# A fused block-sparse attention and feed-forward kernel: one token a partition in the loads of q and k for the later two thirds of batch 0

## The chip, the cores and the metric

The kernel runs on one core of a Trainium2 chip. The core has five engines that run their own instruction streams side by side: TensorE (PE in the profile, with its weight loads as PEld), VectorE (DVE), ScalarE (ACT), GpSimd (POOL) and SyncE (SP), which here only issues DMAs. Sixteen DMA engines move data between the device's memory and the core's on-chip memory (SBUF); TensorE writes its results to a second on-chip memory (PSUM). The metric is device time in microseconds, the median of several runs. A profiled execution of the same program gives the trace.

## The reference

Two parts follow each other. The first is causal attention with block selection over 4 batches, 8 heads, 768 tokens and head size 64: for each token the three best of twelve blocks of 64 keys are chosen by the product of q with the blocks' mean keys, and the token's own block is always in. The second is a feed-forward layer with the tanh form of GELU.

```
k_rep = k.reshape(B, H, n_blocks, block, D).mean(axis=3)
gate_scores = np.einsum('bhsd,bhnd->bhsn', q, k_rep)      # later blocks: -1e9
top_idx = np.argsort(gate_scores, axis=-1)[..., -top_k:]  # top_k = 3, and the own block
scores = scale * np.matmul(q, k.transpose(0, 1, 3, 2))    # masked by block and causally
attn = softmax(scores)
x = (attn @ v), heads side by side                        # 3072 x 512
h = x @ w_in                                              # 512 -> 2048
out = gelu_tanh(h) @ w_out                                # 2048 -> 512
```

The sums of the block means and the choice of blocks need more precision than half precision gives, so q and k also enter in a high and a low half-precision part.

## The kernel before

All work is cut into named steps, and one long list, `ORDER` (L26 to L127), says in which order they are emitted. Each engine runs its own instructions in that order; semaphores hold an instruction until what it reads is there and what it overwrites has been read. A suffix such as `:p`, `:a` or `:v` puts a copy on POOL, ACT or DVE; `@0` to `@2` chooses one of three wide PSUM tiles; `dm4` emits four matmuls without use that keep TensorE's clock up. No planner runs when the program is built: the list is fixed text.

Batch 0 is treated apart from the other three. Its 8 heads form two groups `g` of four heads (two pairs of heads `j` each), and its 768 tokens form three chunks `c` of 256 tokens, each of two token tiles of 128. For chunk 0, `load_first` (L349, steps `d0.g.t.x`) brings q, k and v of one token tile and four heads into a third each of an io tile: partition = token, one run of 64 floats for each head. For chunks 1 and 2, the later two thirds, `load_two` (L365, steps `dd.g.c.x`) brings q (x = 0) or k (x = 1) of all 256 tokens of a chunk in one DMA: partition p gets tokens 2p and 2p + 1, which lie side by side in memory, so that a run is 128 floats. `part` (L386, steps `r.g.c.x`) then copies this on POOL or ACT into a tile of the pool `w32`, sorted by even and odd token. `load_v` (L377, steps `d0.g.t.2`) brings v of one token tile into the last third of one of these io tiles. There are nine io tiles (pool `io`); an io tile is used again when all that it holds has been read.

`t_in` (L432, steps `t2.g.c`) transposes q and k of a chunk on TensorE, eight transposes of 128 x 128, into one wide PSUM tile. For chunks 1 and 2 the even and the odd tokens are written with a stride of two, which puts the tokens in order again. Then `hi` (L451, `h2`, ACT) makes the scaled half-precision copy, `q_low` (`l`, DVE) the low part of q, `k_sum0` and `k_block0` (`s`, `b`, DVE) the block sums, `gate0` and `select0` (`g`, PE; `m`, DVE) the choice of blocks, `mask_t0` and `mask_c0` (`mt`, `mc`) the transposed mask. Scores (`k`, `ma`, PE), exponentials (`x`, ACT), the causal cut (`a`, POOL), the products with v (`p`, PE), their normalisation (`n`, DVE) and the transposes back (`xt`, `xc`) follow for each chunk.

In between, the weights come in: sixteen loads of 512 KB each (`lw.in.s`, `lw.out.s`, L320) into tiles of the pool `w32`, which has seven of 512 KB, each cast to half precision on POOL or DVE (`cw`, L332). The tiles of `part` are from the same pool. The first loads of batches 1 to 3 (`d.4.0`: q of head pair 4; `d.4.1`: k of pair 4) and their half-precision parts (`hn`, `ln`) are in the opening too. The feed-forward layer runs in twelve chunks of 256 tokens: `u` (L931, PE, `hps`), `y` (GELU on ACT), `f` (L965, PE, `ops` and `pso`), `o` and `w` (copy and store). Its matmuls are mixed with the attention of later batches.

SP issues nearly all DMAs, in the order of the list; ACT issues four at the start (k of chunk 0). Eight semaphores serve all DMAs in turn: a DMA waits until the eighth before it has landed, which is why the length of SP's list matters beside its contents.

Of the kernel before, what the change touches and what calls it, by code (L numbers as in the profile page):

```python
# [8 lines left out]
FP32 = mybir.dt.float32  # L9
# [15 lines left out]

ORDER = """  # L26
d0.0.0.0 d0.0.1.0 d0.0.0.1 c.bd c.e0 c.ident d0.0.1.1 c.e.3:p c.gate dd.0.1.0 dd.0.1.1 d0.1.1.0
d0.1.0.0 c.e.2:v d0.1.0.1 r.0.1.0:p dm20 t2.0.0@0 r.0.1.1:p d0.1.1.1 c.m0.0 dd.1.1.0 d0.0.1.2
c.m0.1 c.ident16 h2.0.0 s.0.0 dm14 t2.0.1@1 h2.0.1 b.0.0 dd.1.1.1 l.0.0 s.0.1 g.0.0 c.own t2.1.0@2
h2.1.0 lw.in.5 d0.1.1.2 m.0.0 s.1.0 c.e.1:p dm9 mt.0.0 l.1.0 r.1.1.0:a mc.0.0:a b.1.0 r.1.1.1:p  # L30
c.v.0 k.0.0.0.0@0 dm16 k.0.0.1.0@2 ma.0.0.0 dm3 g.1.0 l.0.1 x.0.0.1.0 d0.0.0.2 m.1.0 dm7 t2.1.1@1
dm8 mt.1.0 a.0.0.1 v.0.0.1:p x.0.0.0.0 a.0.0.0 mc.1.0:a b.0.1 dm8 g.0.1 k.1.0.0.0@2 s.1.1 c.bi
h2.1.1 v.0.0.0:a d0.0.3.2 k.1.0.1.0@0 d0.1.0.2 lw.in.0 cw.in.0:p dd.1.2.0 lw.out.0 ma.1.0.0
x.1.0.1.0 m.0.1 dm16 k.0.1.0.1@0 x.1.0.0.0 c.v.1 dm11 mt.0.1 p.0.0.0@2 p.0.0.1 l.1.1 dd.0.2.0
p.0.0.3 dd.0.2.1 lw.in.4 d0.1.3.2 p.0.0.2 dm3 k.0.1.1.1@1 a.1.0.0 mc.0.1:a a.1.0.1 ma.0.1.1 b.1.1
v.1.0.0:p cw.in.5:p r.0.2.0:p lw.in.7 v.1.0.1:a n.0.0 lw.in.1 g.1.1 r.0.2.1:p x.0.1.0.1 x.0.1.1.1
r.1.2.0:p cw.in.4:p dm7 k.0.1.0.0@0 k.0.1.1.0@2 ma.0.1.0 m.1.1 t2.0.2@1 x.0.1.0.0 s.0.2 dm11 mt.1.1
p.1.0.0@0 p.1.0.2 p.1.0.3 x.0.1.1.0 p.1.0.1 dd.1.2.1 d0.0.2.2 n.1.0 mc.1.1:a k.1.1.1.1@2 cw.in.1:p
dm2 xt.0.0 r.1.2.1:p h2.0.2 lw.out.1 dm9 k.1.1.0.1@0 xc.0.0:a a.0.1.0 lw.in.3 v.0.1.0:p cw.out.0:p
cw.in.3:p l.0.2 ma.1.1.1 lw.in.2 d0.1.2.2 d.4.0 x.1.1.0.1 xt.1.0 x.1.1.1.1 lw.out.2 xc.1.0:v  # L40
t2.1.2@1 cw.in.2:p u.0.0.0@0 u.0.0.1 lw.in.6 lw.out.4 b.0.2 s.1.2 u.0.2.0@2 h2.1.2 l.1.2 g.0.2
b.1.2 u.0.2.1 y.0.0 u.0.1.0@1 m.0.2 u.0.1.1 k.1.1.0.0@0 y.0.2 v.0.1.1:p d.4.1 lw.out.3 v.1.1.0:a
c.par.0 y.0.1 k.1.1.1.0@2 mt.0.2 cw.in.7:p a.0.1.1 a.1.1.1 hn0.4.0:p ma.1.1.0 p.0.1.0@1 p.0.1.2
cw.out.1:p mc.0.2:v ln0.4.0:v p.0.1.3 p.0.1.1 g.1.2 d0.0.4.2 x.1.1.1.0 x.1.1.0.0 f.0.0.0 n.0.1
k.0.2.1.0@1 k.0.2.0.0@2 ma.0.2.0 d.5.0 a.1.1.0 d0.1.4.2 x.0.2.0.0 v.1.1.1:p p.1.1.0@0 m.1.2 p.1.1.2
p.1.1.1 p.1.1.3 xt.0.1 k.0.2.0.1@2 n.1.1 x.0.2.1.0 hn1.4.0:p cw.out.2:p cw.in.6:p cw.out.3:v
xc.0.1:a k.0.2.1.1@1 ma.0.2.1 zql.4.0 mt.1.2 x.0.2.0.1 v.0.2.0:v mc.1.2:v k.0.2.1.2@0 f.0.0.1
xt.1.1 zqh.4.0 u.0.3.0@2 xc.1.1:v x.0.2.1.1 d.5.1 hn0.5.0:p ln1.4.0:v lw.out.6 d0.0.5.2 ln0.5.0:v
k.0.2.0.2@1 ma.0.2.2 u.0.3.1 x.0.2.0.2 lw.out.5 x.0.2.1.2 s.4.0 b.4.0 u.1.0.0@1 u.1.1.0@0
c.ke.0.0:p g.4.0 y.0.3 lw.out.7 u.1.0.1 u.1.1.1 zql.5.0 cw.out.4:v m.4.0 zqh.5.0 zkh.4.0 u.1.2.0@2  # L50
u.1.2.1 hn1.5.0:p a.0.2.1 y.1.0 a.0.2.0 k.1.2.0.0@1 ln1.5.0:v d0.1.5.2 y.1.1 v.0.2.1:a c.ke.0.1:p
cw.out.5:v k.1.2.1.0@0 cw.out.6:p ma.1.2.0 y.1.2 x.1.2.1.0 c.par.1 s.5.0 b.5.0 x.1.2.0.0 p.0.2.0@2
# [78 lines left out]
def kernel(  # L131
# [9 lines left out]
    nc = tc.nc  # L141
    B, H, S, D = q.shape
# [21 lines left out]
    io = ctx.enter_context(tc.tile_pool(name="io", bufs=9))  # L164
    w32p = ctx.enter_context(tc.tile_pool(name="w32", bufs=7))
# [11 lines left out]
    copy_on = {"a": nc.scalar.copy, "v": nc.vector.tensor_copy,  # L177
               "p": nc.gpsimd.tensor_copy}
# [12 lines left out]
    def step(name, f, *args):  # L191
        assert name not in steps, name
        steps[name] = (f, args)
# [3 lines left out]
    ident32 = const.tile([128, 128], FP32)  # L197
# [149 lines left out]
    IO = {}  # L347
# [14 lines left out]
        )  # L362
        IO["v", g, t] = IO["first", g, t][:, 2]

    def load_two(g, c, x):  # L365

        a = io.tile([128, 3, 2, 128], FP32, tag="io", name=f"io_{g}_{c}_{x}")
        nc.sync.dma_start(
            out=a[:, 0:2].rearrange("p a j (h w) -> p (a j h w)",
                                    w=64).rearrange("p (h w) -> p h w", h=4),  # L370
            in_=(q, k)[x][0, 4 * g:4 * g + 4,
                          c * 256:(c + 1) * 256].rearrange(
                "h (p s) d -> p h (s d)", s=2),
        )
        IO["two", g, c, x] = a

    def load_v(g, t):  # L377
        a = IO["two", g, t // 2, t % 2]
        nc.sync.dma_start(
            out=a[:, 2].rearrange("p j (h d) -> p (j h) d", d=D),  # L380
            in_=v[0, 4 * g:4 * g + 4, t * 128:(t + 1) * 128].rearrange(
                "h p d -> p h d"),
        )
        IO["v", g, t] = a[:, 2]

    def part(g, c, x, eng):  # L386

        if ("part", g, c) not in IO:
            IO["part", g, c] = w32p.tile([128, 2, 512], FP32, tag="w32",
                                         name=f"w32_q_{g}_{c}")  # L390
        copy_on[eng](
            out=IO["part", g, c][:, x].rearrange("p (s h d) -> p h s d",
                                                 s=2, d=D),
            in_=IO["two", g, c, x][:, 0:2].rearrange(
                "p a j (h w) -> p (a j h w)", w=64).rearrange(
                "p (h s d) -> p h s d", h=4, d=D))

    def load(p, x):
        b, hp = divmod(p, HP)
# [32 lines left out]
    def t_in(g, c):  # L432

        w = wide.tile([128, 1024], FP32, tag=f"wide{at_slot[0]}",
                      name=f"w_{g}_{c}")
        for x in range(2):
            for j in range(2):
                o = j * 512 + x * 256
                for y in range(2):
                    if c == 0:  # L440
                        to = w[:, o + y * 128:o + (y + 1) * 128]
                        src = IO["first", g, y][:, x, j]
                    else:
                        to = w[:, o:o + 256].rearrange("d (p s) -> d s p",
                                                       s=2)[:, y]
                        src = IO["part", g, c][:, x, y * 256 + j * 128:
                                               y * 256 + (j + 1) * 128]
                    nc.tensor.transpose(to, src, ident32)
        U["w", g, c] = w

    def hi(g, c):  # L451
# [233 lines left out]
    for c in range(NSL2):  # L685
        for g in range(NG):
            un = f"{g}.{c}"
            step(f"t2.{un}", t_in, g, c)
            step(f"h2.{un}", hi, g, c)
            step(f"l.{un}", q_low, g, c)  # L690
            step(f"s.{un}", k_sum0, g, c)
            step(f"b.{un}", k_block0, g, c)
            for y in range(2):
                step(f"v.{un}.{y}", v_copy0, g, c, y)
            step(f"g.{un}", gate0, g, c)
            step(f"m.{un}", select0, g, c)
            step(f"mt.{un}", mask_t0, g, c)
            step(f"mc.{un}", mask_c0, g, c)
            for i in range(c + 1):
                for j in range(2):  # L700
                    step(f"k.{un}.{j}.{i}", score0, g, c, j, i)
                    step(f"x.{un}.{j}.{i}", expo0, g, c, j, i)
                step(f"ma.{un}.{i}", mask_add0, g, c, i)
            for j in range(2):
                step(f"a.{un}.{j}", causal0, g, c, j)
                for hh in range(2):
                    step(f"p.{un}.{2 * j + hh}", pv0, g, c, j, hh)
            step(f"n.{un}", normalise, (g, c), 4, un)
            step(f"xt.{un}", x_t, (g, c), 4, un)
            step(f"xc.{un}", x_c0, g, c)  # L710
# [357 lines left out]
```

## Time and profile before

| | |
|---|---|
| median of 3 runs | 278.28 us (277.52 to 278.75) |
| profiled execution | 277.6 us |
| its span, first to last instruction | 275.0 us |
| PE busy | 261.8 us (95%) |
| ACT, DVE, POOL busy | 190.6, 135.8, 131.3 us |
| mean granted clock of TensorE | 0.994 |
| DMA | 42.65 MB in 114,416 packets |

The page of the profile gives busy time, a picture of the span in forty slices of 6.9 us, the DMA queues, the chain of work that ended last, the costliest groups of instructions and the DMA issues. Further views are read from the trace: the chain in order of time, the instructions of an engine in order of time (start, duration, engine, line, operation, tiles, and in brackets how long the engine was idle before and what released it), the instructions of one line or tile, and tables by window. In such a table a row has the window, its length, and for PE, PEld, DVE, ACT and POOL the busy time and the number of instructions, then the granted clock, the mean busy share of the DMA engines (which may be over 1 as packets overlap) and GB/s. Times in the views are microseconds from the start of the span. An engine's idle time only matters where the chain passes through it.

### The profile page before, as it was taken

The numbers are of one execution on the slowest core, as the hardware profiler recorded it, in microseconds if no ns is written. First come the engines' busy times: TensorE is split into PE (matmuls) and PEld (weight loads), VectorE is DVE, ScalarE is ACT, GpSimd is POOL, SyncE is SP. The second block draws the span as 40 slices with busy tenths as digits, with TensorE's granted clock in tenths as the row PEclk, the third lists the DMA queues.
The fourth block names the chain that finished last, engine by engine and source line by source line (L and its number), as shares of the span: only waits on it lengthen the run. The fifth ranks groups of instructions, "written<-read, shape, count | busy, mean of one in ns | idle before, by whom it ended". The sixth has DMA issues, their size and how long they took to land.

```text
span 275.0 us, 6896 instructions
## 1 busy us (share of the span) xinstructions
PE 261.8 (95%) x2774; PEld 181.4 (66%) x2774; DVE 135.8 (49%) x427; ACT 190.6 (69%) x218; POOL 131.3 (48%) x193
## 2 busy tenths in 40 slices
PE   5889696999999999999999999999999999999995
PEld 3456583774788557795776666786675767756663
DVE  2697359787697776665546456653252110011010
ACT  1568487797889988959899877987978553512321
POOL 6547698899843679673447657600272200000000
PEclk9999799999999999999999999999999999999999
DMA  7999999999799997999996999912205211100203
GB/s 175 274 262 275 336 267 260 224 216 212 140 166 213 201 229 155 170 241 174 147 214 151 204 210 185 223 27 57 69 21 88 69 38 41 38 38 2 76 0 114
DMA packets 114416, 42.65 MB, mean 155 GB/s; under 512 B 102993, under 2 KB 107345, under 8 KB 114385
## 3 DMA queue, kind: packets, MB, share of 16 engines
q1 hardware_dynamic: 112272, 41.70, 72.2%
q10 hardware_dynamic: 2112, 0.52, 1.0%
q8 instruction: 21, 0.34, 0.6%
q14 instruction: 11, 0.08, 0.1%
HBM read 27.26 MB, written 6.29 MB: 122 GB/s over the span
## 4 chain that ended last, share of the span: by engine, by line
PE 74%; DMA 9%; ACT 5%; DVE 4%; POOL 3%; SPq 3%; issue 1%; DVEq 0%; POOLq 0%; ACTq 0%
PE hps L941 27%; PE ops L977 23%; PE st L836 8%; PE pv L878 5%; DMA w_in<-in_moe_w_in_dram 5%; PE pso L977 3%; DMA io<-in_k_dram 3%; DMA io<-in_q_dram 1%; SPq L407 1%; PE mt L814 1%; ACT qk L454 1%; ACT at L852 1%; PE kp L749 1%; PE pv L646 1%; PE gt L778 1%
## 5 line engine op out<-in xcount | busy, mean ns | idle before, releaser
L941 PE MATMUL hps<-xT,w_in 128*128 128x256 f16 x768 | 92.9, 274 | 0.0
L977 PE MATMUL ops<-w_out,gT 128*128 128x512 f16 (+1 forms) x352 | 85.0, 371 | 0.5 <-POOL w_out L338 0.5
L941 PEld LDWEIGHTS <-w_in 128*128 128x128 f16 x768 | 74.6, 98 | 14.9 <-issue 0.2
L852 ACT ACTIVATE at<-st 128x1024 f16<-128x1024 f32 (+1 forms) x72 | 62.8, 917 | 13.2 <-PE st L836 12.0
L951 ACT ACTIVATE gT<-hps 128x1024 f16<-128x1024 f32 x48 | 47.6, 1023 | 28.1 <-PE hps L941 27.7
L977 PEld LDWEIGHTS <-gT 128*128 128x128 f16 x400 | 36.8, 97 | 32.8 <-issue 1.5
L866 POOL TENSOR_SCALAR_AFFINE_SELECT at<-at 128x256 f16<-128x256 f16 x72 | 32.0, 461 | 54.1 <-ACT at L852 53.6
L185 POOL TENSOR_SCALAR hn<-io 128x768 f16<-128x768 f32 x15 | 33.5, 2232 | 9.9 <-DMA io<-in_k_dram 5.5
L836 PE MATMUL st<-qk 76*128 76x128 f16 (+2 forms) x192 | 36.2, 305 | 0.6 <-ACT at L852 0.5
L723 DVE SCALAR_TENSOR_TENSOR ln<-io,hn 128x768 f16<-128x768 f32 x24 | 24.9, 1036 | 3.0 <-POOL hn L185 2.8
L990 DVE COPY osb<-ops 128x512 f32<-128x512 f32 (+1 forms) x7 | 4.4, 632 | 42.7 <-PE ops L977 42.6
L619 ACT ACTIVATE at<-st 128x768 f16<-128x768 f32 (+1 forms) x24 | 20.7, 915 | 6.9 <-PE st L600 6.8
L836 PEld LDWEIGHTS <-qk 76*128 76x128 f16 x192 | 16.6, 97 | 12.2 <-issue 1.1
L878 PEld LDWEIGHTS <-at 128*128 128x128 f16 x504 | 17.3, 97 | 2.5 <-issue 0.4
L878 PE MATMUL pv<-v,at 128*128 128x65 f16 x504 | 17.8, 193 | 0.1
L1016 PE MATMUL dm<-zsrc 128*128 128x512 f16 (+3 forms) x40 | 11.3, 390 | 3.1 <-POOL zsrc L231 3.1
L951 ACT ACT_TABLE_LOAD x11 | 14.1, 1283 | 0.2
L742 POOL COPY qk<-khT 64x768 f16<-64x768 f16 x14 | 11.7, 838 | 1.8 <-DMA khT<-hn 1.3
L657 DVE RECIPROCAL zrec<-pv 128x12 f32<-128x12 f32 x12 | 2.8, 230 | 19.6 <-PE pv L878 19.5
L454 ACT ACTIVATE qk<-w 128x1024 f16<-128x1024 f32 x6 | 6.2, 1029 | 8.2 <-DVE ks L470 4.3
L661 DVE TENSOR_TENSOR xn<-pv,zrec 128x768 f16<-128x768 f32 x12 | 11.5, 957 | 0.4
L823 DVE COPY qk<-mt 12x640 f16<-12x640 f16 x15 | 7.3, 486 | 8.3 <-PE mt L814 8.1
(142 smaller groups left out, 311.9 us busy)
## 6 DMA issues: line engine op xcount, KB each, us to landing
io<-in_q_dram SPq DMA_DIRECT2D x24, 192.0 KB, 4.3
io<-in_k_dram SPq DMA_DIRECT2D x24, 192.0 KB, 3.9
w_in<-in_moe_w_in_dram SPq DMA_DIRECT2D x8, 512.0 KB, 6.3
w_out<-in_moe_w_out_dram SPq DMA_DIRECT2D x8, 512.0 KB, 7.0
out_dram<-osb SPq DMA_DIRECT2D x15, 256.0 KB, 2.6
w_v<-in_v_dram SPq DMA_DIRECT2D x16, 192.0 KB, 4.0
out_dram<-w_o SPq DMA_DIRECT2D x8, 256.0 KB, 2.3
io<-in_v_dram SPq DMA_DIRECT2D x12, 128.0 KB, 5.3
```

What stands on the lines that cost most here:

```text
L185: math_on[eng].tensor_scalar(out=out, in0=in_, scalar1=c, scalar2=None, op0=ALU.mult)
L619: nc.scalar.activation(out=ov, in_=iv, func=AF.Exp, bias=0.0, scale=SCALE / (QS * QS))
L661: nc.vector.tensor_tensor(out=xn[:, 0:nt].rearrange("p c h d -> p h c d"), in0=pz[:, :, :, 0:64], in1=zrec[:, :, 0:nt].unsqueeze(3).to_bro ...
L723: math_on[eng].scalar_tensor_tensor(out=g.rearrange("p t c -> p (t c)"), in0=IO[p, x].rearrange("p t h d -> p (t h d)"), scalar=QS, in1=U[ ...
L742: copy_on[eng](out=dst[0:64, :], in_=U["qh" if x == 0 else "kh", p][64 * hh:64 * hh + 64])
L836: nc.tensor.matmul(st[:, hh, cb:cb + nq * 128], kt[p % 2][hh][0:64 + NBLK, jc * 128:(jc + 1) * 128], qt[p % 2][hh][0:64 + NBLK, qc * 128:( ...
L852: nc.scalar.activation(out=ov, in_=iv, func=AF.Exp, bias=0.0, scale=SCALE / (QS * QS))
L866: nc.gpsimd.affine_select(out=a, in_=a, compare_op=ALU.is_ge, fill=0.0, base=0, pattern=[[0, 2], [1, 128]], channel_multiplier=-1,)
L878: nc.tensor.matmul(U["pv", p][:, o:o + 65], AT[p, hh, jc, qc], v16[p % NSLOT][:, jc, hh, :], start=(jc == 0), stop=(jc == qc),)
L941: nc.tensor.matmul(hps[:, j * TCH:(j + 1) * TCH], w_in16[:, ci, fi * 128:(fi + 1) * 128], xT[:, ci, t0:t0 + TCH], start=(ci == 0), stop=(c ...
L951: nc.scalar.activation(out=g.rearrange("p a w -> p (a w)"), in_=G["h", ch, dj], func=AF.Gelu_apprx_tanh, bias=0.0, scale=1.0,)
L977: nc.tensor.matmul(G["o", ch, ti][:, a:b], G["g", ch, dj][:, j, row * 128:(row + 1) * 128], w_out16[:, fi, a:b], start=(fi == 0), stop=(fi ...
```

## The change

`load_two` now makes one io tile for each token tile: it loads q and then k of one token tile and four heads with two DMAs, one token a partition, as `load_first` does. The steps keep their names: `dd.g.c.y` stands where `dd.g.c.x` stood and loads token tile 2c + y. `load_v` adds v to the same tile. `part`, its eight steps `r.g.c.x` and its four tiles of pool `w32` are gone, and `t_in` reads every chunk from the io tiles and writes it without the stride. The list `ORDER` is the old one without the eight `r` steps. Lines after the list move up by one, those after `part` by nineteen.

```diff
-    def load_two(g, c, x):
-
-        a = io.tile([128, 3, 2, 128], FP32, tag="io", name=f"io_{g}_{c}_{x}")
-        nc.sync.dma_start(
-            out=a[:, 0:2].rearrange("p a j (h w) -> p (a j h w)",
-                                    w=64).rearrange("p (h w) -> p h w", h=4),
-            in_=(q, k)[x][0, 4 * g:4 * g + 4,
-                          c * 256:(c + 1) * 256].rearrange(
-                "h (p s) d -> p h (s d)", s=2),
-        )
-        IO["two", g, c, x] = a
+    def load_two(g, c, y):
+
+        t = 2 * c + y
+        a = io.tile([128, 3, 2, 128], FP32, tag="io", name=f"io_{g}_{t}")
+        for x in range(2):
+            nc.sync.dma_start(
+                out=a[:, x].rearrange("p j (h d) -> p (j h) d", d=D),
+                in_=(q, k)[x][0, 4 * g:4 * g + 4,
+                              t * 128:(t + 1) * 128].rearrange(
+                    "h p d -> p h d"),
+            )
+        IO["first", g, t] = a
 
     def load_v(g, t):
-        a = IO["two", g, t // 2, t % 2]
+        a = IO["first", g, t]
...
-    def part(g, c, x, eng):
-
-        if ("part", g, c) not in IO:
-            IO["part", g, c] = w32p.tile([128, 2, 512], FP32, tag="w32",
-                                         name=f"w32_q_{g}_{c}")
-        copy_on[eng](
-            out=IO["part", g, c][:, x].rearrange("p (s h d) -> p h s d",
-                                                 s=2, d=D),
-            in_=IO["two", g, c, x][:, 0:2].rearrange(
-                "p a j (h w) -> p (a j h w)", w=64).rearrange(
-                "p (h s d) -> p h s d", h=4, d=D))
...
                 step(f"dd.{g}.{c}.{x}", load_two, g, c, x)
-                step(f"r.{g}.{c}.{x}", part, g, c, x)
...
                 for y in range(2):
-                    if c == 0:
-                        to = w[:, o + y * 128:o + (y + 1) * 128]
-                        src = IO["first", g, y][:, x, j]
-                    else:
-                        to = w[:, o:o + 256].rearrange("d (p s) -> d s p",
-                                                       s=2)[:, y]
-                        src = IO["part", g, c][:, x, y * 256 + j * 128:
-                                               y * 256 + (j + 1) * 128]
-                    nc.tensor.transpose(to, src, ident32)
+                    nc.tensor.transpose(
+                        w[:, o + y * 128:o + (y + 1) * 128],
+                        IO["first", g, 2 * c + y][:, x, j], ident32)
```

More of the change, by code (lines that the diff above doesn't have):

```diff
@@ L27 @@
 d0.0.0.0 d0.0.1.0 d0.0.0.1 c.bd c.e0 c.ident d0.0.1.1 c.e.3:p c.gate dd.0.1.0 dd.0.1.1 d0.1.1.0
[L28 to L49, printed above, removed]
+d0.1.0.0 c.e.2:v d0.1.0.1 dm20 t2.0.0@0 d0.1.1.1 c.m0.0 dd.1.1.0 d0.0.1.2 c.m0.1 c.ident16 h2.0.0
@@ new lines @@
+s.0.0 dm14 t2.0.1@1 h2.0.1 b.0.0 dd.1.1.1 l.0.0 s.0.1 g.0.0 c.own t2.1.0@2 h2.1.0 lw.in.5 d0.1.1.2
+m.0.0 s.1.0 c.e.1:p dm9 mt.0.0 l.1.0 mc.0.0:a b.1.0 c.v.0 k.0.0.0.0@0 dm16 k.0.0.1.0@2 ma.0.0.0 dm3
+g.1.0 l.0.1 x.0.0.1.0 d0.0.0.2 m.1.0 dm7 t2.1.1@1 dm8 mt.1.0 a.0.0.1 v.0.0.1:p x.0.0.0.0 a.0.0.0
+mc.1.0:a b.0.1 dm8 g.0.1 k.1.0.0.0@2 s.1.1 c.bi h2.1.1 v.0.0.0:a d0.0.3.2 k.1.0.1.0@0 d0.1.0.2
+lw.in.0 cw.in.0:p dd.1.2.0 lw.out.0 ma.1.0.0 x.1.0.1.0 m.0.1 dm16 k.0.1.0.1@0 x.1.0.0.0 c.v.1 dm11
+mt.0.1 p.0.0.0@2 p.0.0.1 l.1.1 dd.0.2.0 p.0.0.3 dd.0.2.1 lw.in.4 d0.1.3.2 p.0.0.2 dm3 k.0.1.1.1@1
@@ new lines @@
+a.1.0.0 mc.0.1:a a.1.0.1 ma.0.1.1 b.1.1 v.1.0.0:p cw.in.5:p lw.in.7 v.1.0.1:a n.0.0 lw.in.1 g.1.1
+x.0.1.0.1 x.0.1.1.1 cw.in.4:p dm7 k.0.1.0.0@0 k.0.1.1.0@2 ma.0.1.0 m.1.1 t2.0.2@1 x.0.1.0.0 s.0.2
+dm11 mt.1.1 p.1.0.0@0 p.1.0.2 p.1.0.3 x.0.1.1.0 p.1.0.1 dd.1.2.1 d0.0.2.2 n.1.0 mc.1.1:a
+k.1.1.1.1@2 cw.in.1:p dm2 xt.0.0 h2.0.2 lw.out.1 dm9 k.1.1.0.1@0 xc.0.0:a a.0.1.0 lw.in.3 v.0.1.0:p
+cw.out.0:p cw.in.3:p l.0.2 ma.1.1.1 lw.in.2 d0.1.2.2 d.4.0 x.1.1.0.1 xt.1.0 x.1.1.1.1 lw.out.2
+xc.1.0:v t2.1.2@1 cw.in.2:p u.0.0.0@0 u.0.0.1 lw.in.6 lw.out.4 b.0.2 s.1.2 u.0.2.0@2 h2.1.2 l.1.2
@@ new lines @@
+g.0.2 b.1.2 u.0.2.1 y.0.0 u.0.1.0@1 m.0.2 u.0.1.1 k.1.1.0.0@0 y.0.2 v.0.1.1:p d.4.1 lw.out.3
+v.1.1.0:a c.par.0 y.0.1 k.1.1.1.0@2 mt.0.2 cw.in.7:p a.0.1.1 a.1.1.1 hn0.4.0:p ma.1.1.0 p.0.1.0@1
+p.0.1.2 cw.out.1:p mc.0.2:v ln0.4.0:v p.0.1.3 p.0.1.1 g.1.2 d0.0.4.2 x.1.1.1.0 x.1.1.0.0 f.0.0.0
+n.0.1 k.0.2.1.0@1 k.0.2.0.0@2 ma.0.2.0 d.5.0 a.1.1.0 d0.1.4.2 x.0.2.0.0 v.1.1.1:p p.1.1.0@0 m.1.2
+p.1.1.2 p.1.1.1 p.1.1.3 xt.0.1 k.0.2.0.1@2 n.1.1 x.0.2.1.0 hn1.4.0:p cw.out.2:p cw.in.6:p
+cw.out.3:v xc.0.1:a k.0.2.1.1@1 ma.0.2.1 zql.4.0 mt.1.2 x.0.2.0.1 v.0.2.0:v mc.1.2:v k.0.2.1.2@0
@@ L50 @@
+f.0.0.1 xt.1.1 zqh.4.0 u.0.3.0@2 xc.1.1:v x.0.2.1.1 d.5.1 hn0.5.0:p ln1.4.0:v lw.out.6 d0.0.5.2
+ln0.5.0:v k.0.2.0.2@1 ma.0.2.2 u.0.3.1 x.0.2.0.2 lw.out.5 x.0.2.1.2 s.4.0 b.4.0 u.1.0.0@1 u.1.1.0@0
 c.ke.0.0:p g.4.0 y.0.3 lw.out.7 u.1.0.1 u.1.1.1 zql.5.0 cw.out.4:v m.4.0 zqh.5.0 zkh.4.0 u.1.2.0@2
```

## The prediction

> **What bounds the kernel now.** I read the page first (busy times and slices of the span), then the chain of work that ended last in order of time, then the first 50 us engine by engine.
>
> ```profile
> span 275.0 us, 6896 instructions
> PE 261.8 (95%) x2774; PEld 181.4 (66%) x2774; DVE 135.8 (49%) x427; ACT 190.6 (69%) x218; POOL 131.3 (48%) x193
> PE   5889696999999999999999999999999999999995
> DMA packets 114416, 42.65 MB, mean 155 GB/s; under 512 B 102993, under 2 KB 107345, under 8 KB 114385
> ```
>
> PE is busy 95% of the span and its slices are full from the eighth on. So after about 48 us the time is PE's own work, and whatever delays PE before that stays in the total. The change touches loads and copies of the first 31 us; what counts is how late PE comes out of this opening. The chain there:
>
> ```profile
> 10.46 0.94 PE w L448 x8
> ...
> 17.98 1.02 ACT qk L454
> 19.74 6.27 DMA w_in<-in_moe_w_in_dram
> 26.06 1.05 POOL w_in L338
> 27.13 6.53 DMA w_in<-in_moe_w_in_dram
> 33.72 1.05 POOL w_in L338
> ...
> 36.44 7.87 DMA io<-in_k_dram
> 44.46 2.16 POOL hn L185
> ...
> 48.11 1.02 PE ops L977 x4
> ```
>
> Two parts are to be seen. Up to 19.7 us it runs through PE, ACT and DVE (transposes, scaled copies, block sums, gates). From 19.74 to 48.11 it hangs on DMA: two loads of w_in (steps lw.in.4 and lw.in.3), then k of pair 4, each followed by POOL work. POOL's own list says the same, by waits that end with a landing:
>
> ```profile
> 23.27 1.75 POOL L391 COPY w_q<-io 128x512 f32<-128x512 f32 x3
> 26.06 1.04 POOL L338 CAST w_in<-w_in 128x1024 f16<-128x1024 f32 x1 [1.04 <-DMA w_in<-in_moe_w_in_dram]
> 29.27 1.04 POOL L338 CAST w_in<-w_in 128x1024 f16<-128x1024 f32 x1 [2.16 <-DMA w_in<-in_moe_w_in_dram]
> 30.25 0.61 POOL L391 COPY w_q<-io 128x512 f32<-128x512 f32 x1
> ...
> 33.72 1.04 POOL L338 CAST w_in<-w_in 128x1024 f16<-128x1024 f32 x1 [0.94 <-DMA w_in<-in_moe_w_in_dram]
> 35.15 1.04 POOL L338 CAST w_in<-w_in 128x1024 f16<-128x1024 f32 x1 [0.39 <-DMA w_in<-in_moe_w_in_dram]
> ```
>
> SP's queue, with the loads that change (L368) and those behind them:
>
> ```profile
> 1.85 0.50 SPq L368 DMA_DIRECT2D io<-in_q_dram  x1
> 2.40 0.51 SPq L368 DMA_DIRECT2D io<-in_k_dram  x1
> ...
> 19.32 0.37 SPq L368 DMA_DIRECT2D io<-in_k_dram  x1
> 19.74 1.10 SPq L329 DMA_DIRECT2D w_in<-in_moe_w_in_dram  x1
> ...
> 22.52 0.74 SPq L368 DMA_DIRECT2D io<-in_k_dram  x1
> ...
> 27.13 0.88 SPq L329 DMA_DIRECT2D w_in<-in_moe_w_in_dram  x2
> ```
>
> The two loads of the last row are issued within 0.88 us, but their casts at 33.72 and 35.15 start 1.43 us apart, each at a landing: 512 KB in 1.43 us is 367 GB/s. The DMA engines pass loads on one after another, so from 19.7 us a load ahead in the queue delays those behind it by its own transfer time.
>
> **The change part by part.** *Eight copies gone.*
>
> ```profile
> L391 POOL COPY w_q<-io x7: 609/613/636, 6.6 to 30.3; 128x512 f32<-128x512 f32 x7
> L391 ACT COPY w_q<-io x1: 611/611/611, 12.3 to 12.3; 128x512 f32<-128x512 f32 x1
> ```
>
> 8 x 0.61 = 4.9 us of engine time, which I cost at nothing. The three copies from 23.27 end at 25.02, and POOL then waits 1.04 us for a landing. The one at 30.25 stands ahead of the 0.94 us wait. POOL's first three and ACT's one fall before 13 us, where the chain runs through other instructions. Without these waits for DMA as cover, the copy at 30.25 would be worth its 0.61 us.
>
> *Four tiles of the seven-deep w32 pool gone.* Weight loads then wait for older casts, not for transposes. One such wait is on the chain: lw.in.3 starts at 27.13, when the cast of 26.06 has ended (27.11). In the changed order it waits only for the landing of lw.in.4 (26.01), so it could be issued up to 1.1 us earlier. It lands behind what is queued all the same; nothing gained, unless the queue is not the limit.
>
> *Eight loads of 256 KB become sixteen of 128 KB.* The bytes stay, the runs shrink from 512 B to 256 B: an old load (4 heads by 128 partitions) is 512 packets, its two successors 1024; 4096 packets more in all. Stages by window (the last three columns are granted clock, DMA share, GB/s):
>
> ```profile
> 18.00:21.00 3.00, 2.49 (x29) 1.13 (x26) 2.39 (x15) 2.70 (x4) 1.31 (x4) 1.00 0.71 219
> 12.50:14.50 2.00, 1.70 (x20) 0.65 (x19) 1.93 (x6) 0.68 (x3) 0.28 (x3) 1.00 1.32 241
> 21.00:21.50 0.50, 0.50 (x16) 0.48 (x14) 0.00 (x0) 0.20 (x1) 0.50 (x2) 1.00 1.11 324
> 27.24:30.65 3.41, 1.55 (x22) 0.88 (x20) 1.55 (x5) 2.04 (x4) 1.38 (x2) 1.00 1.10 333
> 30.65:34.06 3.41, 3.14 (x15) 2.47 (x16) 0.89 (x2) 1.24 (x2) 2.47 (x5) 0.50 1.06 346
> 40.90:44.30 3.40, 2.16 (x34) 0.92 (x30) 3.33 (x12) 2.13 (x3) 2.58 (x3) 1.00 1.13 306
> ```
>
> In the second row mostly v loads in 256 B runs arrive (241 GB/s: 0.54 us for 128 KB), in the third an old load in 512 B runs (324 GB/s: 0.81 us for 256 KB). So a pair takes 1.09 us for 0.81 us: 0.28 us more. Bounds: nothing, if the load is limited elsewhere; and another 0.81 us, if a packet costs the same at either size. I take 0.28, the two rows being of this very traffic.
>
> The Trainium skill (DMA: Bandwidth & Descriptors, section Why small descriptors are slow) counts three extra cycles for each packet beside one for 32 bytes: 11 cycles for 256 B, 19 for 512 B, so a pair would take 22/19 = 1.16 times the old load. The estimate by that page is 0.13 us on the 0.81 us, and the sum below would be 0.63 instead of 0.78; the rows here show 1.35 times.
>
> Where it falls: six of the eight loads go out before 19.32. The first row of windows shows the DMA engines at a share of 0.71: between 18 and 21 us the queue runs dry, since SP holds back the loads of 16.32 and 19.32 until an io tile is free. What the six pairs add (6 x 0.28 = 1.7 us) is worked off there. Costed at nothing; with no dry stretch it would be up to 1.7.
>
> Behind 19.32 SP now issues two loads before lw.in.4 (the load there becomes q and k of token tile 5). One more issue is 2.40 - 1.85 = 0.55 us by SP's spacing, 0.42 by 19.74 - 19.32. I take 0.50, and all of it is on the chain, because the queue is short there and lw.in.4's landing follows its issue. The pair at 22.52 stands in the full queue ahead of lw.in.3, lw.in.2 and k of pair 4: 0.28 more. **Sum: 0.50 + 0.28 = 0.78 us, taken as 0.8.** POOL's casts then start at 26.6, 34.5 and 35.9, hn at 45.2, and PE's ops at 48.9.
>
> *The transposes.* Read from io tiles directly, with the same count and size. One place matters:
>
> ```profile
> 28.16 0.63 PE L448 MATMUL w<-ident,w_q 128*128 128x128 f32 x4
> 30.92 1.12 PE L448 MATMUL w<-ident,w_q 128*128 128x128 f32 x4 [2.13 <-POOL w_q L391]
> ...
> DMA to landing us min/median/max: 7.5/7.5/7.5
> ```
>
> The last row is the load of 22.52: k lands at 30.0, POOL copies it until 30.86, PE goes on at 30.92. In the changed kernel the second transpose already wants q of token tile 5, so seven of the eight wait, until 30.0 + 0.78 = 30.8. PE resumes as before, but with three transposes more at the halved clock of 30.65 to 34.06 (1.12/4 = 0.28 each): up to 0.8 us late. This lies beside the 0.8 us by which the w_in casts come later, which PE's next work needs; it is not added.
>
> *The first loads of group 1.* Before, its last q load went out at 4.2 and took 5.3 us:
>
> ```profile
> L356 SPq DMA_DIRECT2D io<-in_q_dram x1: 368/368/368, 4.2 to 4.2; - x1
> DMA to landing us min/median/max: 5.1/5.2/5.3
> ```
>
> So it landed at 9.5, and its transposes start at 10.46 on the chain: 0.9 us to spare. Two old loads stand ahead of it, which become four: 2 x 0.28 = 0.56 us later. SP and ACT also wait there for the landing of the eighth DMA before, which now binds all four of group 1's loads. ACT's sequencer is held at these issues, ahead of its first scaled copy. I take nothing; bounds 0 and 0.8.
>
> **The rivals.**
>
> *A second halved clock (slower).* With 1.55 us of PE work in the window 27.24:30.65 the granted clock fell to 0.50 in the next; with 2.16 us in 40.90:44.30 it stayed at 1.00. If PE's waits in that later window grow by 0.6 us or more, it comes down to the first's figure, and a half-speed window of 3.41 us costs 1.7: 278.3 + 0.8 + 1.7 = 280.8. Against it: PE enters that window late as well. The Trainium skill (TensorE: Matmul & The Clock Gate, Part 1) has a free-running window of 3.4 us and a halved clock after an idle one; the length agrees with the 3.41 us here, but by an idle window alone the drop at 30.65 would not have come, with 1.55 us of work before it.
>
> *Group 1's loads late (slower).* If they are over 0.9 us late, the whole chain from 10.46 moves; up to 0.8 more: 279.9.
>
> *Nothing seen (same).* Loads limited by issue and latency, the extra issue lost in SP's waits: 278.3.
>
> *The copies were the bound (faster).* PE's wait at 30.92 was ended by POOL's copy. If the pair of 22.52 lands by 30.0 as before, PE goes on 0.9 us earlier, window 27.24:30.65 gets 2.2 us of work, as much as the one that kept its clock, and the halved window (half of 3.14 = 1.6 us) is saved, with lw.in.3's 1.1 us beside it: 276.7. It decides only if the pair is no later than the single load; the 7.5 us which that load took in a full queue speaks against.
>
> **How the numbers follow.** The profiled execution took 277.6 us (span 275.0 and 2.6 around it), within the three runs (277.52 to 278.75, median 278.28). The sum gives 278.4 against the profiled one and 279.1 against the median. Half a per cent, 1.4 us, is about what the measurement can tell from no change, so "slower" starts at 279.7. Chances: the forecast 0.55 (278.7 to 279.9, with 0.18 of it above 279.7), second halved clock 0.14, group 1 late 0.12, nothing seen 0.09, faster 0.10. Together: faster 0.10, same 0.37 + 0.09 = 0.46, slower 0.18 + 0.14 + 0.12 = 0.44. The range takes in all but the faster case and the upper tail: 277.9 to 281.0.
>
> **What would show it.** Right: 118,512 packets; two L369 issues from 19.3 and w_in's about 20.3; POOL's casts, hn and PE's ops at the times above, with PE waiting before its transposes near 30.8 for DMA, not POOL. Wrong: casts no later than 33.7 and 35.2 (the queue was not the limit), a second stretch of clock 0.50 after 40 us, or transposes of group 1 starting well after 10.5.

## The result, and the profile after

The changed kernel takes 280.92 us (median; 279.3 to 282.87) and the one before, on the same chip, 277.85 (276.33 to 281.34). The ratio is 1.010, 95% interval 1.0081 to 1.0119: 2.3 to 3.3 us slower, where 0.8 was forecast. The profiled execution took 279.8 us. Executions of one kernel lie 3 to 5 us apart, so a single profile shows where time goes, and only the medians say how much. The mean granted clock of the changed kernel lay between 0.982 and 0.994 in its twenty executions, so a row about the clock holds for one execution alone.

From the page of the changed kernel: the span, PE's busy time and the packets.

```profile
span 278.1 us, 6893 instructions
PE 262.5 (94%) x2774; PEld 182.3 (66%) x2774; DVE 135.7 (49%) x427; ACT 190.2 (68%) x217; POOL 126.7 (46%) x186
DMA packets 118639, 42.65 MB, mean 153 GB/s; under 512 B 111312, under 2 KB 111568, under 8 KB 118608
```

The bytes are the same, the packets 4223 more (4096 were forecast), the copies are off POOL (126.7 us for 131.3), and PE is busy for 0.7 us more. The rest of the 3.1 us by which the span grew is idle time of PE. Its chain of work in order of time shows that they arise in the opening:

```profile
20.36 2.48 SPq L328
25.64 1.79 SPq L379
27.47 2.06 SPq L328
29.58 6.87 DMA w_in<-in_moe_w_in_dram
39.25 7.66 DMA io<-in_k_dram
47.06 2.13 POOL hn L184
```

The landings on it are those that the prediction named, lw.in.3 and k of pair 4. What is new is that SP's own issuing (SPq) stands on the chain from 20.36 us. SP's queue in order of time (start, duration, line, operation):

```profile
19.80 0.51 SPq L369 DMA_DIRECT2D io<-in_k_dram  x1
20.36 2.48 SPq L328 DMA_DIRECT2D w_in<-in_moe_w_in_dram  x1
...
24.98 0.61 SPq L369 DMA_DIRECT2D io<-in_k_dram  x1
...
27.47 2.06 SPq L328 DMA_DIRECT2D w_out<-in_moe_w_out_dram  x1
29.58 1.90 SPq L328 DMA_DIRECT2D w_in<-in_moe_w_in_dram  x2
```

lw.in.4 is issued 0.62 us later than before, as forecast, but the issue itself lasts 2.48 us for 1.10, and what follows goes out 2 to 2.5 us late: k of the last pair at 24.98 for 22.52, lw.in.3 at 29.58 for 27.13. POOL's casts and hn, and PE, by the same view of their engines:

```profile
27.36 1.04 POOL L337 CAST w_in<-w_in 128x1024 f16<-128x1024 f32 x1 [3.96 <-DMA w_in<-in_moe_w_in_dram]
...
36.50 1.04 POOL L337 CAST w_in<-w_in 128x1024 f16<-128x1024 f32 x1 [1.85 <-DMA w_in<-in_moe_w_in_dram]
37.96 1.04 POOL L337 CAST w_in<-w_in 128x1024 f16<-128x1024 f32 x1 [0.42 <-DMA w_in<-in_moe_w_in_dram]
...
47.06 2.13 POOL L184 TENSOR_SCALAR hn<-io 128x768 f16<-128x768 f32 x1 [0.78 <-DMA io<-in_k_dram]
```

```profile
10.36 1.09 PE L427 MATMUL w<-ident,io 128*128 128x128 f32 x8
...
28.21 0.28 PE L427 MATMUL w<-ident,io 128*128 128x128 f32 x1
32.15 1.76 PE L427 MATMUL w<-ident,io 128*128 128x128 f32 x7 [3.67 <-DMA io<-in_q_dram]
...
50.50 1.04 PE L958 MATMUL ops<-w_out,gT 128*128 128x512 f16 x4
```

The casts of 33.72 and 35.15 now stand at 36.50 and 37.96 (2.8 later), hn at 47.06 for 44.46 (2.6 later), PE's ops at 50.50 for 48.11 (2.4 later). What the DMA engines moved goes with it. In these tables by window the last three columns are granted clock, DMA share and GB/s. Before:

```profile
0.00:18.00 18.00, 13.30 (x109) 8.14 (x111) 10.22 (x37) 6.83 (x10) 10.14 (x34) 1.00 1.02 238
...
21.00:24.00 3.00, 2.99 (x62) 1.76 (x60) 2.01 (x12) 2.19 (x4) 3.00 (x6) 1.00 0.90 218
24.00:30.00 6.00, 4.79 (x65) 3.23 (x57) 4.18 (x10) 5.12 (x7) 2.79 (x4) 1.00 1.07 335
30.00:36.00 6.00, 5.08 (x45) 4.25 (x46) 1.97 (x5) 3.17 (x3) 4.67 (x7) 0.72 1.05 298
...
0.00:36.00 36.00, 28.64 (x295) 18.51 (x296) 20.77 (x77) 20.01 (x27) 21.91 (x51) 0.95 1.00 261
```

After:

```profile
0.00:18.00 18.00, 12.95 (x107) 8.15 (x109) 10.02 (x36) 6.29 (x8) 8.26 (x30) 1.00 1.08 211
18.00:21.00 3.00, 2.49 (x27) 1.13 (x28) 2.75 (x16) 2.73 (x4) 1.34 (x4) 1.00 1.02 295
21.00:24.00 3.00, 2.99 (x63) 1.83 (x60) 1.94 (x12) 2.19 (x4) 2.40 (x4) 1.00 0.81 167
24.00:30.00 6.00, 4.49 (x62) 2.93 (x54) 3.50 (x10) 5.12 (x7) 1.04 (x1) 1.00 1.00 282
30.00:36.00 6.00, 3.85 (x18) 3.16 (x19) 0.96 (x2) 1.31 (x2) 3.01 (x4) 0.55 1.02 297
...
0.00:36.00 36.00, 26.76 (x265) 17.20 (x266) 19.18 (x74) 17.64 (x25) 16.04 (x42) 0.93 1.03 240
```

GB/s times microseconds gives kB. By 36 us the changed kernel has moved (261 - 240) x 36 = 756 kB less, which at the 298 GB/s of the stage before it are 2.5 us, about the lateness of the casts. By stage: at 18 us (238 - 211) x 18 = 486 kB are missing. In the pause of 18 to 21 us it does catch up, (295 - 219) x 3 = 228 kB, but from 21 to 24 it loses 153 again and from 24 to 30 another 318; from 30 on it moves as much as before. So the pause takes about half of what was missing, and what is missing at 36 us is for the larger part lost behind it. From 21 to 24 us there is a new pause (share 0.81). SP is held there at lw.in.4 until 22.84 and sends nothing behind it; whether this hold is the cause of the second loss is a question for the experiments.

### The profile page after: what moved, and what is told of

Same layout as the page of the kernel before. It is cut to its first block, busy times and chain, and to the rows that moved or that the text cites. A ratio compares the mean times of both kernels' runs of the same rounds, so it can differ in the third digit from the quotient of the medians.

```text
span 278.1 us, 6893 instructions
## 1 busy us (share of the span) xinstructions
PE 262.5 (94%) x2774; PEld 182.3 (66%) x2774; DVE 135.7 (49%) x427; ACT 190.2 (68%) x217; POOL 126.7 (46%) x186
## 4 chain that ended last, share of the span: by engine, by line
PE 71%; DMA 7%; ACT 6%; POOL 6%; SPq 4%; DVE 3%; issue 2%; POOLq 0%; DVEq 0%; ACTq 0%
PE hps L922 25%; PE ops L958 22%; PE st L817 9%; PE pv L859 6%; DMA io<-in_k_dram 4%; PE pso L958 3%; DMA w_in<-in_moe_w_in_dram 2%; SPq L328 2%; POOL w_out L337 1%; ACT qk L435 1%; POOL qk L723 1%; ACT at L833 1%; PE mt L795 1%; PE w L427 1%; ACT L833 1%
## 5 line engine op out<-in xcount | busy, mean ns | idle before, releaser
L337 POOL CAST w_in<-w_in 128x1024 f16<-128x1024 f32 x8 | 8.8, 1098 | 11.0 <-DMA w_in<-in_moe_w_in_dram 11.0
L613 POOL TENSOR_SCALAR_AFFINE_SELECT at<-at 128x512 f16<-128x512 f16 x12 | 9.0, 762 | 8.2 <-ACT at L600 8.1
```

The costliest lines, as they stand in the source:

```text
L337: copy_on[eng](out=dst, in_=w_parts[which, s])
```

## The experiments

The main theory is that short runs move fewer bytes in a microsecond, that nearly all loads of the opening go through one queue with almost no pause to spare, and that lateness at 36 us becomes time. Against it stand the number of DMAs, the missing copies and tiles, PE's wait for the last pair, and the halved clock. Times are ratios to the kernel before on the same chip; 0.1% is 0.28 us.

**Each chunk alone.**

```diff
+                if c == 1:      # c1_only; c == 2 in c2_only
+                    step(f"dd.{g}.{c}.{x}", load_one, g, c, x)   # one token a partition
+                else:
                     step(f"dd.{g}.{c}.{x}", load_two, g, c, x)
                     step(f"r.{g}.{c}.{x}", part, g, c, x)
```

> The change in chunk 1 alone (four of the eight loads become pairs, four copies and two w32 tiles go); chunk 2 as before. Theory (the DMA queue carries lateness from chunk 1 into the w_in loads): +0.9 to +1.9 us, 1.2 as the value, and the w_in cast that stood at 26.06 starts 0.7 to 1.3 us later. Rival (what counts is the pair right ahead of the w_in loads, and what chunk 1 adds is worked off while SP waits for io tiles, as the prediction had it): within 0.3 us of before.

> The change in chunk 2 alone (steps dd.0.2 and dd.1.2, the last four loads). Theory: the extra issue and the pair in the full queue remain, +0.8 to +1.6 us; together with the chunk 1 run about the whole 3 us, or less than it if the second stretch of halved clock needs both. Rival (the prediction's place): nearly the whole difference, +2.5 to +3 us.

c1_only: 278.04 us, ratio 1.0002 (0.9966 to 1.0038). c2_only: 279.54, 1.0056 (1.0016 to 1.0095). The earlier chunk alone costs nothing that can be told, against what was expected of it; the rival, which is the prediction's own step, held. The later chunk alone costs 1.6 us (0.4 to 2.6). The two intervals overlap, so it is likely, but not shown, that the later chunk costs more. The windows of c1_only:

```profile
0.00:18.00 18.00, 13.19 (x107) 8.16 (x109) 10.00 (x36) 6.29 (x8) 8.29 (x30) 1.00 1.07 210
18.00:21.00 3.00, 2.49 (x28) 1.16 (x28) 2.82 (x15) 2.73 (x4) 1.30 (x4) 1.00 1.00 319
21.00:24.00 3.00, 2.99 (x63) 1.83 (x60) 2.44 (x13) 2.19 (x4) 3.00 (x5) 1.00 1.02 303
0.00:36.00 36.00, 28.68 (x287) 18.37 (x288) 21.82 (x77) 19.64 (x26) 19.38 (x47) 0.95 1.04 259
```

At 18 us (238 - 210) x 18 = 504 kB are missing, with four pairs as many as in the changed kernel with six. The pause takes (319 - 219) x 3 = 300 kB and the next 3 us another (303 - 218) x 3 = 255, and at 36 us only (261 - 259) x 36 = 72 kB are missing. So it is not the backlog at 18 us that tells the two kernels apart, but what happens from 21 us on. SP's issue of lw.in.4, in c1_only and then in c2_only:

```profile
19.85 0.50 SPq L329 DMA_DIRECT2D w_in<-in_moe_w_in_dram  x1
```

```profile
20.91 0.51 SPq L329 DMA_DIRECT2D w_in<-in_moe_w_in_dram  x1
```

With the pairs of one chunk SP is not held at lw.in.4; with those of both it is, for 2.48 us. The sum of the two ratios, 0.6%, is less than the 1.0% of both, as a backlog that only both together build up would have it, though the intervals don't exclude equality. The bytes at 36 us are not the whole account: c2_only moves 257 GB/s until then, so 144 kB or 0.5 us are missing, and part of its loss stands later, in a wait of PE:

```profile
64.22 0.39 PE L599 MATMUL st<-qk 64*128 64x256 f16 x4 [1.28 <-DVE xn_0.2_1262 L678]
```

On the chain of c2_only this wait stands behind a load of w_out that lands at 60.55 us. The profiled execution of c1_only, with 280.21 us one of its two longest, has such a wait too (1.02 us); those of the kernel before and of the changed one have none there.

c2_only has another use: its granted clock is full from 20 to 274 us.

```profile
20.00:274.00 254.00, 245.34 (x2643) 171.34 (x2643) 123.81 (x380) 181.99 (x207) 116.20 (x153) 1.00 0.73 148
```

The kernel before has a halved stretch in that span and is faster, so a lost window of clock does not make the difference. The mean granted clocks of all executions say the same. One halved window of 3.41 us takes 0.006 off the mean. Of 111 executions of the kernel before that were taken beside the experiments, the 19 at 0.999 and 1.000 have a median of 278.1 us, the 65 at 0.992 to 0.994 have 277.9, and the 27 at 0.987 and 0.988 have 278.8. The changed kernel's four at 0.993 and 0.994 have 281.7, its fourteen at 0.987 and 0.988 have 280.6: it is slower by 1.8 us or more at the same clock.

**More DMAs with the old runs, and the copies away with the old loads.** issues_x2 cuts each of the eight loads into two by pair of heads; copies_only lets the transposes read the two-token io tiles as they are; it leaves the sorting out, so that its tokens stand in another order.

```diff
+        for j in range(2):                                   # issues_x2
             nc.sync.dma_start(
+                out=a[:, j]..., in_=(q, k)[x][0, 4 * g + 2 * j:4 * g + 2 * j + 2, ...]
-                step(f"r.{g}.{c}.{x}", part, g, c, x)        # copies_only
...
+                        src = IO["two", g, c, x][:, j, y]
```

> Before, with each of the eight loads cut into two DMAs of two heads each (128 KB, runs of 512 B): as many issues as in the changed kernel, as many packets as before, copies kept. Theory (packets of 256 B are what slows the queue): +0.3 to +1.0 us, from one more issue of 0.5 us ahead of the w_in load. Rival (the number of DMAs is what counts: eight semaphores in turn, SP's issue time): +2 to +3 us, as the changed kernel.

> Before with the eight sort copies and their four w32 tiles taken out and the loads of two tokens kept; the transposes read the io tiles unsorted, so that the tokens and head sizes stand in another order than they should. Prediction's step: 0 (within 0.3 us of before), as POOL then waits for a landing. Rival (the copies were the bound of the transposes at 30.92): 0.9 to 1.6 us faster, and no stretch of halved clock.

issues_x2: 278.5, 1.0014 (0.9987 to 1.0042). copies_only: 277.56, 0.9989 (0.9954 to 1.0024). Eight issues more cost between -0.4 and 1.2 us (its issue of lw.in.4 lasted 1.41 us); the copies and their tiles together are worth between -0.7 and 1.3 us, a gain that can't be told from none.

**Short runs alone.** runs_256 keeps the copies and all tiles, and loads each half by token tile:

```diff
-        nc.sync.dma_start(out=a[:, 0:2]..., in_=... "h (p s) d -> p h (s d)", s=2)
+        for s in range(2):
+            nc.sync.dma_start(
+                out=a[:, s].rearrange("p j (h d) -> p (j h) d", d=D),
+                in_=(q, k)[x][0, 4 * g:4 * g + 4,
+                              c * 256 + s * 128:c * 256 + (s + 1) * 128
+                              ].rearrange("h p d -> p h d"))
```

> The kernel before with its eight copies and all its w32 tiles kept; only its eight loads are each cut in two by token tile, so that they move in sixteen loads with 256 B runs, as in the changed kernel. If the short runs are the cause, the time is that of the changed kernel: 0.7 to 1.2% above before (280.0 to 281.3), with lw.in.4's issue held over 2 us again. If the missing copies and tiles were part of the cause, it stays within 0.3% of before. Sixteen loads with 512 B runs cost 0.14% (not told from nothing).

280.6 us, ratio 1.0073 (1.0046 to 1.0101), 2.0 us. The issue of lw.in.4 and the first 36 us, from its queue and its table by window:

```profile
20.71 2.50 SPq L329 DMA_DIRECT2D w_in<-in_moe_w_in_dram  x1
```

```profile
0.00:36.00 36.00, 26.48 (x260) 16.26 (x261) 19.57 (x73) 17.11 (x25) 20.22 (x49) 0.95 1.01 244
```

SP is held as in the changed kernel, and (261 - 244) x 36 = 612 kB are missing, 2.05 us at 298 GB/s. Against issues_x2 it is the length of the runs that differs (and that the copies and the transposes' output no longer stride). The runs are therefore most of the loss; whether the remaining 0.3% is anything is not told, as the two intervals overlap.

**Which wait carries it.** Three versions of the changed kernel, each with one relief: lw.out.0 later in the queue, the last pair earlier, idle matmuls that keep the clock up.

```diff
-... dd.1.2.0 lw.out.0 ma.1.0.0 ...            # after_late: lw.out.0 moved
+... dd.1.2.1 lw.out.0 d0.0.2.2 ...
-... p.1.0.1 dd.1.2.1 d0.0.2.2 ...             # after_swap: dd.1.2.1 moved
+... cw.in.5:p dd.1.2.1 lw.in.7 ...
-xc.1.0:v t2.1.2@1 ...                         # after_dm
+xc.1.0:v dm16 t2.1.2@1 ...
```

> The changed kernel with lw.out.0 (512 KB, not needed before 40 us) moved in SP's order from ahead of dd.0.2.0 to behind dd.1.2.1. If the queue is still full when lw.in.4 is issued at 20.4 us, this takes 512 KB (1.4 to 2 us) out of it: lw.in.4's issue is held under 1.3 us, its cast comes at 26 or before, the q and k that PE waits for land 1 to 2 us earlier, and 0.8 to 2 us of the 2.8 come back (ratio to before 1.002 to 1.007). If the queue was empty by then (as the prediction had it), nothing changes: ratio 1.010.

> The changed kernel with the pair dd.1.2.1 (q and k of token tile 5, group 1) ahead of lw.in.7 and lw.in.1 in SP's order, 1 MB earlier in the queue. If PE's wait for this pair at 28.5 to 32.2 us is what costs, it shrinks by 2 us or more, the clock's halved stretch is at most one window, and 1.5 to 2.8 us come back (ratio to before 1.000 to 1.005). If the casts of w_in are the bound, they come 0.7 us later for the pair ahead of them, and the ratio stays at 1.008 to 1.012.

> The changed kernel with four idle matmuls of 512 columns (some 0.9 us at the full clock) ahead of PE's last transposes of group 1, where PE waits anyhow; no load moves. If the halved clock from 30.6 us is a cost of its own (5.3 us of PE's work at half speed), PE's work in the window before it rises from 1.5 to 2.4 us, the clock stays at 1.00 there, and 1 to 2.6 us come back (ratio to before 1.001 to 1.006). If the landings alone set the pace, PE waits longer for the next casts instead, and the ratio stays at 1.008 to 1.012.

after_late: 280.1, 1.0053 (1.0022 to 1.0083). SP's issue of lw.in.4, and PE:

```profile
20.65 0.51 SPq L327 DMA_DIRECT2D w_in<-in_moe_w_in_dram  x1
```

```profile
30.19 1.00 PE L426 MATMUL w<-ident,io 128*128 128x128 f32 x7 [1.66 <-DMA io<-in_q_dram]
...
39.23 3.46 PE L921 MATMUL hps<-xT,w_in 128*128 128x256 f16 x16 [4.15 <-POOL w_in L336]
```

With 512 KB less in front SP is no longer held, as with the pairs of one chunk: the hold comes with what is queued ahead. But without it the DMA engines still move only 183 GB/s from 21 to 24 us, with those 512 KB moved behind, and half of the loss stays; so the hold is not shown to be the whole cause. PE goes on at 30.19, earlier than in the kernel before, and then waits 4.15 us for a cast of w_in, because lw.out.0 now stands ahead of lw.in.3. after_swap: 279.82, 1.0054 (1.0021 to 1.0087), between the two outcomes that were expected of it; PE's transposes don't wait at all, and the cast is waited for instead:

```profile
28.79 1.04 PE L426 MATMUL w<-ident,io 128*128 128x128 f32 x8
...
34.75 0.61 PE L921 MATMUL hps<-xT,w_in 128*128 128x256 f16 x2 [4.69 <-POOL w_in L336]
```

The order in the queue decides at which instruction PE waits, and brings back about half of the loss (0.5% of 1.0%). after_dm: 281.76, 1.0119 (1.0078 to 1.016), nothing comes back:

```profile
27.84:31.25 3.41, 1.87 (x22) 0.85 (x21) 1.42 (x5) 1.83 (x3) 0.65 (x1) 1.00 1.04 302
31.25:34.67 3.42, 1.26 (x10) 0.99 (x11) 0.02 (x1) 0.00 (x0) 1.92 (x4) 1.00 0.99 260
34.67:38.08 3.41, 3.41 (x19) 2.41 (x17) 1.79 (x5) 2.51 (x3) 1.04 (x3) 0.50 1.03 317
```

PE's work in the first window (third column) rose from 1.28 us in the changed kernel to 1.87, and the next window kept its clock; but that next one holds the wait itself, and the one after it is halved. The edit moved the halved window rather than removing it, so it is no clean test of the clock; c2_only and the list of clocks are the better ones.

**The weights out of the way.** after_out moves lw.out.0 and lw.out.1 behind lw.in.2 in the changed kernel, before_out in the one before.

```diff
-... dd.1.2.0 lw.out.0 ... h2.0.2 lw.out.1 ... cw.out.0:p cw.in.3:p ... lw.in.2 d0.1.2.2 ...
+... dd.1.2.0 ... h2.0.2 ... cw.in.3:p ... lw.in.2 lw.out.0 lw.out.1 d0.1.2.2 ... cw.in.7:p cw.out.0:p
```

> The changed kernel with lw.out.0 and lw.out.1 (512 KB each) moved in SP's order behind lw.in.2, and the cast of the first moved on POOL behind cw.in.7; PE first reads them at 41 to 44 us. If the transfers queued ahead of lw.in.3 and lw.in.2 set the time, 1 MB less ahead of them (some 2.8 us at 367 GB/s) brings their casts from 36.5 and 38.0 to 33.7 to 35.5, and 1.5 to 2.8 us come back: ratio to before 1.000 to 1.005. If PE's wait for the last pair of q and k is the cost by itself, the ratio stays at 1.008 to 1.012, also if the two weights then come too late for PE's down products.

> The same move in the kernel before. There lw.in.3 waits at 27.13 for a tile that the cast of 26.06 frees, so only the 512 KB of lw.out.1, issued shortly ahead of it, and what of lw.out.0 is still in the queue can be gained. If the transfers ahead of the casts set the time: 0.5 to 1.5 us faster, ratio 0.994 to 0.998. If they don't: 0.998 to 1.002, or slower by PE's wait for the two moved weights.

Both expectations failed: after_out 281.93, 1.0163 (1.0106 to 1.0221); before_out 279.67, 1.0049 (1.0021 to 1.0078). In before_out the casts come 1.7 us earlier (32.06 and 33.42), but k of pair 4 comes later, and with it hn, which stands on POOL ahead of the cast of lw.out.2:

```profile
46.41 2.13 POOL L184 TENSOR_SCALAR hn<-io 128x768 f16<-128x768 f32 x1 [3.25 <-DMA io<-in_k_dram]
```

```profile
50.03 1.38 PE L976 MATMUL ops<-w_out,gT 128*128 128x512 f16 x4 [1.87 <-POOL w_out L337]
```

There are two landings to serve, w_in at 34 us and k of pair 4 at 44; time won at the first was lost at the second. The prediction had read them as one chain.

**As many bytes away as the packets cost, and both landings relieved.** after_less and before_less halve three weight loads; the casts read the half that comes twice, so that the other half of these weights is left out. after_both and before_both move dd.1.2.1 ahead of lw.in.7 and d.4.1 ahead of lw.out.2.

```diff
+        if (which, s) in (("in", 0), ("out", 0), ("in", 4)):      # after_less, before_less
+            nc.sync.dma_start(out=t[:, 0:1], in_=src[:, 0:1])
+            t = t[:, 0:1].to_broadcast([128, 2, 512])
...
-... d.4.0 ... lw.out.2 ... d.4.1 ...              # after_both, before_both: beside dd.1.2.1
+... d.4.0 d.4.1 ... lw.out.2 ...
```

> The changed kernel, whose loads lw.in.0, lw.out.0 and lw.in.4 bring only the first half of their weights (256 KB each for 512); the casts read this half twice, so a part of the expert products is computed from repeated weights. 768 KB are some 2.1 us of transfer at the 367 GB/s of the profile before, and 4096 shorter packets cost about as much (8 x 0.28 = 2.2 us). If the transfer time of all that stands ahead of the casts and of k of pair 4 sets the time, it comes back: ratio to before 0.999 to 1.004. If the number of issues, or the order of them, sets it: 1.008 to 1.012.

> The same three half loads in the kernel before. If its opening too is paced by transfers all along (no slack for eight times 0.28 us anywhere), it gains about what the changed kernel gains: ratio 0.991 to 0.996. If the pause of 18 to 21 us gives slack, so that only what stands behind it counts, it gains at most the quarter MB of lw.in.4: ratio 0.997 to 1.000.

> The changed kernel with two loads moved ahead in SP's order: the pair dd.1.2.1 ahead of lw.in.7, and q and k of pair 4's second load (d.4.1) behind d.4.0, ahead of lw.out.2. The first alone gave 1.0054, with PE late again at 49 us, behind POOL's hn that waits for d.4.1. If that wait is the second limit of the same late queue, both together give 0.996 to 1.003. If the pace of the casts of w_in sets it, nothing is added: 1.004 to 1.008; if SP has to wait for an io tile at d.4.1, it is slower than 1.008.

> The same two moves in the kernel before (there the pair is one load). If PE's opening is limited by the landing of these two, 0.992 to 0.998. If the casts of w_in set it, 0.998 to 1.004.

after_less: 278.32, 1.001 (0.9982 to 1.0039). before_less: 277.77, 0.9971 (0.9944 to 0.9998). The first 36 us and the pause of after_less, then of before_less:

```profile
0.00:36.00 36.00, 28.74 (x302) 18.66 (x302) 23.18 (x87) 20.49 (x27) 16.94 (x43) 1.00 1.03 233
18.00:21.00 3.00, 2.49 (x31) 1.17 (x28) 2.88 (x14) 2.73 (x4) 1.25 (x4) 1.00 1.08 275
```

```profile
0.00:36.00 36.00, 28.81 (x279) 18.19 (x280) 20.98 (x77) 20.09 (x27) 21.99 (x51) 0.95 0.93 240
18.00:21.00 3.00, 2.49 (x34) 1.20 (x31) 2.65 (x16) 2.73 (x4) 1.19 (x3) 1.00 0.35 98
```

Three halves are 786 kB, 2.6 us at 298 GB/s. In the changed kernel they bring back 2.5 us (1.010 to 1.001), and what is missing at 36 us falls from 756 to (261 - 233) x 36 - 786 = 222 kB. In the kernel before they bring 0.8 us (0.1 to 1.6): there the pause grows (98 GB/s for 219, 363 kB), as SP still waits for its io tiles until 19.6. So bytes taken away from the kernel before mostly lengthen its pause, while what runs_256 has not moved by 36 us comes out at the end nearly in full (2.05 us by bytes, 2.0 measured). By these runs the kernel before stands just short of where the queue limits it. The expectation for before_less, at most the quarter MB of lw.in.4, holds within its interval.

after_both: 279.32, 1.0046 (1.0019 to 1.0073), no better than after_swap. before_both: 277.89, 0.9981 (0.9952 to 1.001), not told from the kernel before. No order of the queue that was tried beats the kernel before beyond its interval.

## Why the prediction was wrong

The sum was 0.50 + 0.28 + 0, and the term costed at zero was the large one.

- **"What the six pairs add is worked off there. Costed at nothing."** This step failed. The row it rested on, a DMA share of 0.71 in 3 us, has room for (1 - 0.71) x 3 = 0.87 us; the six pairs were put at 1.7. In the changed kernel 486 kB were missing at 18 us (1.6 us at 298 GB/s), 228 kB or 0.77 us of it were made up in the pause, and 471 kB were lost anew from 21 to 30 us, so that 2.5 us were missing at 36. With the pairs of the earlier chunk alone (c1_only) the step holds, though as many bytes were missing at 18 us, and the working off goes on behind the pause. So the size of the pause is not the whole fault. The step took the pause for a gap of the DMA engines alone and did not ask what follows it: with the pairs of both chunks queued, SP was held 2.48 us at lw.in.4 (0.50 and 0.51 with those of one chunk), what stood behind went out 2 to 2.5 us later, and a new pause opened from 21 to 24. What share of the second loss is the hold's is not shown. The upper bound that the prediction gave and laid aside, 1.7 with no dry stretch, makes the sum 2.5; measured 2.3 to 3.3. That it fits is in part luck, since it charges each pair alike and the four of c1_only cost nothing alone.
- **A pair costs 0.28 us.** Right in size over all eight: eight times 0.28 is 2.2 us, runs_256 gave 2.0 (1.3 to 2.8). No run shows it pair by pair. The Trainium skill (DMA: Bandwidth & Descriptors, Why small descriptors are slow) gives by its three extra cycles a packet, 22 to 19 for a pair and its old load, 8 x 0.13 = 1.0 us, an estimate by that page; it lies below the measured interval.
- **One more issue, 0.50 us.** lw.in.4 went out 20.36 - 19.74 = 0.62 us later, so the step holds at that place. What was overlooked is that the issue itself can get longer: 2.48 us for 1.10.
- **Eight copies, four tiles: nothing.** copies_only agrees with zero (-0.7 to 1.3 us of gain). The rival in which the copies were the bound falls.
- **Group 1's first loads: nothing.** Its transposes start at 10.36, for 10.46 of the chain before. The rival falls.
- **PE waits for DMA, not POOL, near 30.8.** Right in kind, late by 1.3 us (32.15), as the pair was issued 2 to 2.5 us late. "Wrong if a second stretch of clock 0.50 after 40 us" did not occur, but the first stretch lasted two windows, which the prediction had not thought of. The rival of a second halved clock, with 280.8, came near the measured time by luck: after_late and c2_only have PE at full clock where the changed kernel has not, and PE then waits 4.15 us for the casts, or the kernel is 0.6% slower all the same; and by the list of clocks above a lost window goes with less than 1 us. The halved stretch lies beside the wait for landings, as the prediction said of its three transposes.
- **One chain to 48 us.** Too simple. before_out, after_out and after_swap show at least two landings that limit in turn.

Left open: how much of the second loss, from 21 to 30 us, SP's hold makes, and why the changed kernel moves only 282 GB/s from 24 to 30 us (335 before), as its loads there differ in kind and in when SP sent them; and whether the loss by the missing tiles, or by PE's dependence on two pairs, is more than zero.

## What to carry to other kernels

A pause in the use of an engine is room of a size: share missing times length, compared with what is to go in. It is only a first estimate, since working off can go on behind the pause (c1_only) or a new pause can open there (the changed kernel), if whoever feeds that engine, here SP, can't send. Where most transfers of an opening share one queue, test the parts of a change alone and together: here one part cost nothing that could be told, the other 0.6%, and both 1.0%. Before trusting that a wait is the cost, relieve it: here PE only waited at the next instruction.

## What the runs showed of the hardware

- SP's issue of lw.in.4 (512 KB) took 0.50, 0.51 and 0.51 us (c1_only, c2_only, after_late), 1.10 (before), 1.41 (issues_x2) or 2.48 and 2.50 us (changed, runs_256). With 512 KB less ahead of it in the queue, 2.48 became 0.51.
- The clock is halved after a window in which PE worked some, but little: 1.26 us of 3.42 was followed by 0.50, 1.87 of 3.41 was not (after_dm). The Trainium skill (TensorE: Matmul & The Clock Gate, Part 1) tells of an idle window; here a window more than a third busy did it, and the windows' length agrees (3.41 us).
